# Linear attention and a two-layer network in one kernel: batch 0's numerator and denominator computed with tokens in rows, scaled there, and turned by PE

## The chip, the cores and the metric

The kernel runs on one core of a Trainium2 chip. The metric is the device time of one execution in microseconds (us). In the profile the engines are PE (matrix products; PEld is its loading of weights), DVE (element-wise work), ACT (activation functions and copies), POOL (here mostly the issue of loads) and SP (the issue of stores and of transposing transfers).

## The reference, cut to what matters

There are 8 batches of 8 heads with 576 tokens of 64 features. With phi(x) = max(x,0) + min(exp(x),1):

```python
q_p, k_p = phi(q), phi(k)
kv  = einsum('bhsd,bhse->bhde', k_p, v)
z   = sum(k_p, axis=2)
num = einsum('bhsd,bhde->bhse', q_p, kv)
den = einsum('bhsd,bhd->bhs', q_p, z)[..., None] + 1e-06
x   = (num / den), tokens in rows, heads side by side: 4608 x 512
h   = x @ w_in            # 512 x 2048
out = (h - tanh(h)) @ w_out   # 2048 x 512, float32
```

## The kernel before, in words

The order of all instructions is written out by hand; each engine runs its own list in order, and semaphores make one engine wait for another.

**Chunks and slots.** The two layers run over nine chunks of 512 tokens. For chunk `c`, layer 1 makes 16 blocks `fi` of 128 hidden features (`l1mm`, L430, four matmuls of 128x512 each, over the four pairs of heads that the 512 features of x fall into). ACT takes tanh (`th`) and DVE subtracts it, which gives `gT`. Layer 2 (`l2mm`, L451) follows in 16 slots `s` of four matmuls each. The lists `s1[fi]` and `s2[s]` hold the work of the attention that is put in behind a block or a slot, so that PE computes the attention of the next batch between the matmuls of the layers. A chunk of 512 tokens is not a batch of 576: chunk 1 begins with the last 64 tokens of batch 0 and goes on with batch 1.

**Opening.** Batch 0 has nothing to hide behind. POOL issues its loads as six halves (two halves of heads `i` for each of q, k and v), in the order q, q, k, k, v, v (L89), then w_in and w_out. For each half of q and k the phi takes three instructions (`phi_pieces`): ACT's exp `e`, DVE's `r` = max(x,0)+1, and DVE's minimum of the two, which gives `qp` or `kp`. PE turns qp (`a_qT_pe`, L166, PE transposes through PSUM; ACT and DVE each copy a part to `qT`). Then `b0_z` (L252) sums kp, `b0_kv` (L263) makes kv, and both are copied into `kz` (`b0_kz`, L267). `a_den` (L333, L337) makes den, with 1e-6 put in by matmuls with the tile `eps`; DVE takes the reciprocal (L346). `num_mm` (L273) makes num for 512 tokens with features in rows, which is how layer 1 reads x; ACT copies it to `ns` (L293). Since a den belongs to a token, hence to a column, `b0_spread` (L300) spreads the reciprocals over the rows with 32 matmuls in float32, and DVE multiplies (`b0_scale`, L304) into `xT`. Layer 1 of chunk 0 starts with the first four blocks in matmuls of 256 tokens (L686), first all four pairs on tokens 0 to 255, then on 256 to 511. `spin` (L532) multiplies zeros on PE where PE would otherwise stand still.

**The last 64 tokens of batch 0** are not needed in chunk 0. `rest_mm` (L281) and `scale_rest` (L324) make them later, in slot 8, with reciprocals that SP sends through DRAM and back (`spread_rest`).

**Batch 1** is made in layer 2 of chunk 0: phi of q at slots 0 and 1, phi of k at 4 and 5, the PE transposes at 5, `kv1` (`a_kv` L184, `a_kz`) at 8, `a_den` and `num1` (L273, L610) and the split of the reciprocals (`a_split`) at 9, `spread1` (L419, L423, four scales of 128x512) at 12. The tile `ps_all` is the whole PSUM, eight banks of 512 float32 columns; the code names banks by number.

Of the kernel before, what the change touches and what calls it, by code (L numbers as in the profile page):

```python
# [11 lines left out]
F32 = mybir.dt.float32  # L12
# [6 lines left out]
def kernel(  # L19
# [33 lines left out]
    ps_all = psum.tile([128, 8, 512], F32, name="ps_all")  # L53

# [10 lines left out]
    sel = const.tile([128, NP, 2, 64], F32, name="sel")  # L65
# [5 lines left out]
    one = const.tile([128, J * 16], BF16, name="one")  # L71
    eps = const.tile([128, 32], BF16, name="eps")
# [11 lines left out]
    def load(b, t, src, halves):  # L84

        x = src[b].rearrange("h (p j) d -> (h p) (j d)", j=J)
        if halves:
            for i in range(2):
                nc.gpsimd.dma_start(out=t[:, :, i].rearrange("q h j d -> q h (j d)"),  # L89
                                    in_=x.rearrange("(h i q) x -> i q h x", h=2, i=2)[i])  # L90
        else:
            nc.gpsimd.dma_start(out=t.rearrange("q h i j d -> q (h i) (j d)"),  # L92
                                in_=x.rearrange("(n q) x -> q n x", n=4))

    def load_k(b):
        k_t[b] = kpool.tile([128, 2, 2, J, D], BF16, name="kraw")
        load(b, k_t[b], k, b == 0)

    def load_q(b):
        q_t[b] = kpool.tile([128, 2, 2, J, D], BF16, name="qraw")  # L100
        load(b, q_t[b], q, b == 0)

    def load_v(b):
        load(b, v_b[b % 2][:, 0:2], v, b < 2)
# [45 lines left out]
    def new_qT(b):  # L150
        qT_t[b] = work.tile([128, 2, J, 2, 64], BF16, name="qT")
# [7 lines left out]
    def a_qT_pe(b, i, banks, on=None):  # L159
        if i == 0:  # L160
            new_qT(b)
        for n in range(2):
            j0, j1 = ((0, 5), (5, 9))[n]
            ps = banks().bitcast(BF16).rearrange("p (j t) -> p j t", t=128)
            for j in range(j0, j1):
                nc.tensor.transpose(ps[:, j - j0, :], qp_t[b][:, i, j].rearrange("p h d -> p (h d)"), ident)  # L166
            src = ps[:, 0:j1 - j0, :]
            dst = qT_t[b][:, i, j0:j1].rearrange("p j g t -> p j (g t)")
            if (on or "AV")[n] == "A":
                nc.scalar.copy(dst, src)  # L170
            else:
                nc.vector.tensor_copy(dst, src)
# [76 lines left out]
    def b0_z(i):  # L249

        for j in range(J):
            nc.tensor.matmul(ps_all[:, 5 - 3 * i, 0:2], kp_t[0][:, i, j].rearrange("p h d -> p (h d)"), two,  # L252
                             start=(j == 0), stop=(j == J - 1))

    def b0_zc(i):
        nc.vector.tensor_mul(kz_t[0][:, :, i, 64:96],
                             ps_all[:, 5 - 3 * i, 0:2].unsqueeze(2).to_broadcast([128, 2, 32]), mask[:, :, i, :])
# [26 lines left out]

    def b0_num(i):

        b0 = 2 * i
        num_mm(0, i, lambda h: b0 + h)

    def b0_evac(i, ns):  # L290

        b0 = 2 * i
        nc.scalar.copy(ns[:, i::2, 0:8, :].rearrange("p a j t -> p a (j t)"), ps_all[:, b0:b0 + 2, :])  # L293

    def b0_spread(pairs, n0):

        for n, p in enumerate(pairs):
            for t in range(4):
                r = slice(32 * t, 32 * t + 32)
                nc.tensor.matmul(ps_all[:, 4 + t, 128 * (n0 + n):128 * (n0 + n) + 128],  # L300
                                 sel[r, p].rearrange("p h e -> p (h e)"), rden_t[0][r, 0:128], start=True, stop=True)

    def b0_scale(p, ns, n, j0=0, j1=8):
        nc.vector.tensor_mul(  # L304
            xT[:, p, 64 * j0:64 * j1].rearrange("p (j t c) -> p t j c", j=j1 - j0, t=4),
            ns[:, p, j0:j1].rearrange("p j (t c) -> p t j c", t=4),
            ps_all[:, 4:8, 128 * n + 16 * j0:128 * n + 16 * j1].rearrange("p t (j c) -> p t j c", c=16))
# [20 lines left out]
    def a_den(b, bank, parts=range(4)):  # L328

        kz, qT = kz_t[b], qT_t[b]  # L330
        ps = ps_all[:, bank, 0:J * 16]
        for t in range(4) if b == 0 else ():
            nc.tensor.matmul(ps[32 * t:32 * t + 32], eps[:, 0:32], one[:, 0:J * 16], start=True, stop=False)  # L333
        for n, p in enumerate((0, 2, 1, 3)):
            if n in parts:
                for t in range(4):
                    nc.tensor.matmul(ps[32 * t:32 * t + 32], kz[:, p // 2, p % 2, 64:96],  # L337
                                     qT[:, p % 2, :, p // 2, 16 * t:16 * t + 16],
                                     start=(n == 0 and b > 0), stop=(n == NP - 1))
        if b > 0:  # L340
            den = rpool.tile([128, J * 16], F32, name="den")
            nc.vector.tensor_scalar(den, ps, 1e-6, None, ALU.add)
        else:
            den = ps
        rden = rpool.tile([128, J * 16], F32, name="rden")
        nc.vector.reciprocal(rden, den)  # L346
        rden_t[b] = rden
# [108 lines left out]
    def evac(c, i, o, f0=0, f1=None):  # L456
# [13 lines left out]
        def store():  # L470
            for half in range(2):
                b, j = divmod(2 * (4 * c + i) + half, J)
                cuts = [f0, 256, f1] if c == 3 else [f0, f1]
                for a0, a1 in zip(cuts, cuts[1:]):
                    nc.sync.dma_start(  # L475
                        out=out[b * S:(b + 1) * S, a0:a1].rearrange("(p j) m -> p j m", j=J)[:, j, :],
                        in_=osb[64 * half:64 * half + 64, a0:a1])
# [10 lines left out]
    load_q(0)  # L488
    make_identity(nc, ident)
    load_k(0)  # L490
    load_v(0)
# [21 lines left out]
    nc.vector.memset(one, 1.0)  # L513
# [3 lines left out]
    nc.vector.memset(eps, 0.0)  # L517
    rest = 1e-6
    for n in range(3):
        e0 = float(np.float32(rest).astype(ml_dtypes.bfloat16))  # L520
        nc.vector.memset(eps[32 * n:32 * n + 1], e0)
        rest -= e0


    for t in range(4):
        nc.vector.tensor_copy(s8[32 * t:32 * t + 32, 0].rearrange("q h p -> q (h p)"),
                              ident[32 * t:32 * t + 32, 32 * t:32 * t + 8])
    nc.vector.tensor_copy(sel, s8[:, 0].rearrange("q h p -> q p h").unsqueeze(3).to_broadcast([128, NP, 2, 64]))

    def spin(n):  # L530
        for _ in range(n):
            nc.tensor.matmul(ps_all[:, 0, :], zero[:, 0:128], zero, start=True, stop=True)  # L532
# [4 lines left out]
    for f in (eq0, rq0, mq0, eq1, rq1, mq1):  # L537
        f()
    spin(18)
    a_qT_pe(0, 0, side, "AV")  # L540
    (ek0, rk0, mk0), (ek1, rk1, mk1) = (phi_pieces(0, k_t, kp_t, "kp", i, 2 * i) for i in range(2))
    for f in (ek0, rk0):
        f()
    spin(5)
    a_qT_pe(0, 1, side, "AV")
    for f in (*ek1, mk0, rk1):
        f()
    spin(6)
    b0_z(0)
    spin(3)  # L550
    for f in mk1:
        f()
    b0_zc(0)
    b0_kv(0)
    b0_z(1)
    b0_zc(1)
    b0_kz(0)
    a_den(0, 4)
    ns0 = new_ns(0)
    spread_rest(0)  # L560
    b0_num(0)
    b0_kv(1)
    b0_kz(1)
    b0_evac(0, ns0)
    b0_num(1)
    b0_evac(1, ns0)
    b0_spread((0, 2, 1, 3), 0)
    for x in range(2):
        for n, p in enumerate((0, 2, 1, 3)):
            b0_scale(p, ns0, n, 4 * x, 4 * x + 4)  # L570

    def prepare():

        for t in range(4):
            nc.vector.tensor_copy(s8[32 * t:32 * t + 32, 1:3].rearrange("q n h p -> q (n h p)"),
                                  ident[32 * t:32 * t + 32, 32 * t + 8:32 * t + 24])
# [9 lines left out]
    for c in range(NC):  # L586
# [4 lines left out]
        if c == 0:  # L591
# [7 lines left out]
            def kv1():  # L599
                a_kv(1, 4)  # L600
                pss = rest_mm(0, 4, 256)
                a_kz(1, 4)
                scale_rest(0, pss)
# [10 lines left out]
            s2[4].append(lambda: a_kphi(1, 0))  # L614
            s2[5].append(lambda: (a_qT_pe(1, 0, Banks([4, 5])), a_qT_pe(1, 1, Banks([6, 7])), a_kphi(1, 1),
                                  load_q(2), load_k(2), load_v(2)))
            s2[2].append(prepare)
            s2[8].append(kv1)
            s2[9].append(lambda: (a_den(1, 4), num1(), spread_rest(1), a_split(1)))
            s2[12].append(spread1)  # L620
# [57 lines left out]
        if c == 0:  # L678

            first = Banks([4, 5, 6, 7, 0, 1, 2, 3])  # L680
            hs = [ps_all[:, n, :] for n in range(4)]
            for x in range(2):
                xs = slice(256 * x, 256 * x + 256)
                for n, p in enumerate((0, 2, 1, 3)):
                    for fi in range(4):
                        nc.tensor.matmul(hs[fi][:, xs], w_in_sb[:, p, fi * 128:(fi + 1) * 128], xT[:, p, xs],  # L686
                                         start=(x == 0 and n == 0), stop=(x == 1 and n == 3))
            for fi in range(4):
                l1act(fi, hs[fi], gT)
        for fi in range(4 if c == 0 else 0, NF):  # L690
            h = first() if c == 0 else ps_all[:, fi % 6, :]
            if c == 2 and fi == 1:
# [5 lines left out]
            elif c != 2 or fi > 1:  # L698
# [65 lines left out]
```

## Time and profile before

| | |
|---|---|
| Time, median of three runs | 284.41 us (284.24 to 284.88) |
| The profiled execution: its own time | 284.32 us |
| The profiled execution: span from first to last instruction | 282.6 us |
| Around the span | 1.72 us |
| PE busy | 277.0 us of the span |
| DVE, ACT busy | 176.1 and 145.6 us |
| First real matmul of layer 1 (L686) starts | 16.82 us |
| Last PE work in the chain ends | 269.00 us |

The page's first part gives the busy time of each engine. The chain of waits goes back from the last instruction to what released each step; in order of time it shows what the end hung on. A row of the timeline has start, duration, engine, line, operation, result and operand with partitions x elements, count, and in brackets the idle time before it and what ended that. A duration includes the latency of an instruction, so that in a series one starts before the one ahead has ended: the spacing is then the series' length divided by its count.

### The profile page before, as it was taken

The page shows a single profiled execution, that of the slowest core. Times are in us where ns is not written, and L with a number is a line of the kernel's source. Part 1 is how long each engine was busy: PE and PEld are TensorE (multiplying, and loading weights), DVE is VectorE, ACT ScalarE, POOL GpSimd, SP SyncE. Part 2 cuts the span into 40 slices and gives each one's busy share as a digit, 9 for nine tenths or more (in the row PEclk, how much of TensorE's full clock was granted, in tenths as well). Part 3 has the DMA queues.
Part 4 walks back from the last instruction along what each step waited for, and adds up shares of the span by engine and source line. Part 5 has one row for each costly group of instructions (what it writes and reads, how often), then busy time and mean ns, then how long its engine had stood idle before and what let it go on. Part 6 is the DMA issues. An engine that isn't in the chain of part 4 may idle for free.

```text
span 282.6 us, 5093 instructions
## 1 busy us (share of the span) xinstructions
PE 277.0 (98%) x2084; PEld 131.9 (47%) x2084; DVE 176.1 (62%) x283; ACT 145.6 (52%) x176; POOL 77.5 (27%) x69
## 2 busy tenths in 40 slices
PE   8989999999999999999999999999999999999995
PEld 3564454454444454445444444444444444444443
DVE  5859977984779773977397639764870167006600
ACT  3648647946346753566366735572651365126411
POOL 8653120430361526233614360506050000000000
PEclk9999999999999999999999999999999999999999
DMA  6999999899994399049903792252115210230032
GB/s 103 199 207 212 205 207 209 172 192 197 236 237 76 71 194 217 5 84 162 220 22 73 115 240 60 48 110 48 29 22 123 58 32 2 57 79 13 2 74 75
DMA packets 38743, 33.12 MB, mean 117 GB/s; under 512 B 16160, under 2 KB 34624, under 8 KB 38592
## 3 DMA queue, kind: packets, MB, share of 16 engines
q0 software_dynamic: 17504, 18.35, 40.1%
q1 hardware_dynamic: 21216, 14.45, 21.8%
q8 instruction: 16, 0.26, 0.3%
q14 instruction: 7, 0.06, 0.1%
HBM read 38.14 MB, written 9.46 MB: 168 GB/s over the span
## 4 chain that ended last, share of the span: by engine, by line
PE 90%; DMA 5%; POOL 1%; ACT 1%; issue 1%; SPq 0%; DVE 0%; DVEq 0%; POOLq 0%
PE ps_all L430 43%; PE ps_all L451 41%; DMA v<-in_v_dram 3%; DMA out_dram<-osb 3%; PE ps_all L184 2%; PE ps_all L273 2%; PE ps_all L686 1%; ACT osb L462 1%; SPq L475 0%; POOL kraw L89 0%; PE ps_all L337 0%; POOL qraw L89 0%; PE ps_all L300 0%; PE ps_all L166 0%; PE ps_all L263 0%
## 5 line engine op out<-in xcount | busy, mean ns | idle before, releaser
L451 PE MATMUL ps_all<-w_out_sb,gT 128*128 128x512 bf16 x560 | 124.6, 379 | 0.0
L430 PE MATMUL ps_all<-xT,w_in_sb 128*128 128x512 bf16 x560 | 122.7, 379 | 0.0
L437 DVE TENSOR_TENSOR gT<-ps_all,th 128x1024 bf16<-128x1024 f32 x64 | 77.8, 1218 | 46.4 <-ACT th L436 46.4
L436 ACT ACTIVATE th<-ps_all 128x1024 f32<-128x1024 f32 x64 | 65.5, 1024 | 46.9 <-PE ps_all L430 46.9
L430 PEld LDWEIGHTS <-w_in_sb 128*128 128x128 bf16 x560 | 54.6, 98 | 65.5
L451 PEld LDWEIGHTS <-gT 128*128 128x128 bf16 x560 | 53.8, 98 | 63.2 <-issue 0.2
L462 ACT COPY osb<-ps_all 128x512 f32<-128x512 f32 (+1 forms) x36 | 20.7, 582 | 56.4 <-PE ps_all L451 40.0
L245 POOL TENSOR_TENSOR qp<-qp,rd 128x1152 bf16<-128x1152 bf16 x10 | 21.0, 2118 | 39.1 <-issue 23.7
L231 POOL TENSOR_TENSOR pr<-qp,zb 128x1152 f32<-128x1152 bf16 x10 | 23.5, 2362 | 21.6 <-ACT zb L224 21.6
L236 DVE TENSOR_REDUCE dn<-pr 128x9 f32<-128x576 f32 x20 | 14.5, 745 | 12.2 <-POOL pr L231 12.2
L136 ACT ACTIVATE e<-qraw 128x1152 bf16<-128x1152 bf16 x16 | 18.5, 1161 | 5.4 <-DMA qraw<-in_q_dram 5.4
L136 ACT ACTIVATE e<-kraw 128x1152 bf16<-128x1152 bf16 x15 | 17.4, 1162 | 1.9 <-DMA kraw<-in_k_dram 1.9
L138 DVE TENSOR_TENSOR qp<-e,r 128x1152 bf16<-128x1152 bf16 x16 | 12.1, 759 | 4.4 <-ACT e L136 3.3
L92 POOL DMA_DIRECT2D kraw<-in_k_dram x7 | 5.4, 769 | 33.1 <-DVE r L137 17.7
L138 DVE TENSOR_TENSOR kp<-e,r 128x1152 bf16<-128x1152 bf16 x15 | 11.4, 763 | 4.4 <-ACT e L136 3.5
L441 ACT ACTIVATE th<-ps_all 128x512 f32<-128x512 f32 x16 | 9.4, 597 | 5.5 <-PE ps_all L686 3.7
L442 DVE TENSOR_TENSOR gT<-ps_all,th 128x512 bf16<-128x512 f32 x16 | 10.4, 687 | 2.7 <-ACT th L441 1.7
L532 PE MATMUL ps_all<-zero 128*128 128x512 bf16 x32 | 10.1, 475 | 1.2 <-DVE zero L485 1.2
L92 POOL DMA_DIRECT2D qraw<-in_q_dram x7 | 5.2, 741 | 16.7 <-ACT e L136 7.3
L137 DVE TENSOR_SCALAR r<-qraw 128x1152 bf16<-128x1152 bf16 x16 | 7.4, 465 | 0.4 <-DMA qraw<-in_q_dram 0.4
L460 DVE COPY osb<-ps_all 128x128 f32<-128x128 f32 x1 | 0.3, 292 | 11.6 <-DMA out_dram<-osb 11.6
L199 DVE COPY vp<-v 128x1152 bf16<-128x1152 bf16 x10 | 5.3, 525 | 3.2 <-DMA v<-in_v_dram 3.2
(105 smaller groups left out, 141.1 us busy)
## 6 DMA issues: line engine op xcount, KB each, us to landing
out_dram<-osb SPq DMA_DIRECT2D x62, 128.0 KB, 2.5
qraw<-in_q_dram POOLq DMA_DIRECT2D x7, 576.0 KB, 10.5
kraw<-in_k_dram POOLq DMA_DIRECT2D x7, 576.0 KB, 7.8
v<-in_v_dram POOLq DMA_DIRECT2D x6, 576.0 KB, 11.4
w_in_sb<-in_moe_w_in_dram POOLq DMA_DIRECT2D x3, 512.0 KB, 13.1
w_out_sb<-in_moe_w_out_dram POOLq DMA_DIRECT2D x3, 512.0 KB, 16.3
v<-in_v_dram POOLq DMA_DIRECT2D x4, 288.0 KB, 12.9
rdb<-ds SPq DMA_DIRECT2D x2, 576.0 KB
```

The costliest lines, as they stand in the source:

```text
L92: nc.gpsimd.dma_start(out=t.rearrange("q h i j d -> q (h i) (j d)"), in_=x.rearrange("(n q) x -> q n x", n=4))
L136: return (lambda: nc.scalar.activation(e, x, AF.Exp), lambda: nc.vector.tensor_scalar(r, x, 0.0, 1.0, ALU.max, ALU.add), lambda: nc.vector ...
L138: lambda: nc.vector.tensor_tensor(y, e, r, ALU.min))
L231: nc.gpsimd.tensor_mul(pr_t[b][:, i].rearrange("p j h d -> p j (h d)"), qp_t[b][:, i].rearrange("p j h d -> p j (h d)"), zb_t[b][:, i].uns ...
L236: nc.vector.tensor_reduce(dn_t[b][:, i, :, h], pr_t[b][:, i, :, h, :], mybir.AxisListType.X, ALU.add)
L245: nc.gpsimd.tensor_mul(x, x, rd[:, i].unsqueeze(2).to_broadcast([128, J * 2, D]))
L430: nc.tensor.matmul(h, w_in_sb[:, p, fi * 128:(fi + 1) * 128], xT[:, p, c * 512:(c + 1) * 512], start=(n == 0), stop=(n == NP - 1))
L436: nc.scalar.activation(th, h, AF.Tanh)
L437: nc.vector.tensor_sub(gT[:, fi:fi + 2, :], h, th)
L442: nc.vector.tensor_sub(gT[:, fi, :], h, th)
L451: nc.tensor.matmul(o, gT[:, fi, i * 128:(i + 1) * 128], w_out_sb[:, fi, :], start=(fi == 0), stop=(fi == NF - 1))
L462: nc.scalar.copy(osb[:, f0:f1], o[:, f0:f1])
```

## The change

Four things change together.

1. **Loads and phi by halves of heads.** The loads come as q, k, v of the first half, then q, k, v of the second half. `phi`, z, kv and num of the first half precede those of the second half on every engine.
2. **Batch 0's num with tokens in rows.** The matmul's weights are now 128 tokens of `qT` (whose layout for batch 0 is changed so that they lie side by side), and the moving side is 65 columns of `kz`: 64 of kv and one of z. So den comes out as the 65th column, in the same row as its token. DVE adds 1e-6, takes the reciprocal of eight numbers for each row and multiplies (`b0_scale`, four DVE instructions for two units of 128 tokens of a half of heads) into `xk`. PE turns `xk` back to features in rows (`b0_turn`, four transposes), and ACT copies to `xT` (`b0_out`). The tiles `sel`, `one`, `eps`, the reciprocal of 128x144, the spread and `ns` of batch 0 go. The first blocks of layer 1 become four parts: first half of heads, then second half. The last 64 tokens are made in the same way (`b0_rest`, `b0_rest_turn`), without DRAM.
3. **Batch 1 one slot later**: kv1 at slot 9, num1 at 10, spread1 at 13, but the PE transposes one slot earlier, at 4. Ahead of num1, in the same slot, stands `b0_rest_turn`. Chunk 1 gets the order of its first two blocks that chunk 2 had: pairs 0 and 1 for both, then pairs 2 and 3.
4. **Small**: fewer zero matmuls (25 for 32), the last block of chunk 3 is stored in two parts in place of four, batch 1's v is loaded by halves as before.

The core of the diff:

```diff
+    def tok_mm(i, js, m, bank, o):
+        for hg in range(2):
+            for h in range(2):
+                rs = slice(64 * h, 64 * h + 64)
+                nc.tensor.matmul(ps_all[0:m, bank + h, o + 65 * hg:o + 65 * hg + 65], qT_t[0][rs, i, hg, js].rearrange("p j t -> p (j t)"),
+                                 kz_t[0][rs, hg, i, 0:65], start=True, stop=True)
+    def tok_recip(m, bank, o, n):
+        d = rpool.tile([128, 2, 4], F32, name="d")[0:m, :, 0:n]
+        nc.vector.tensor_scalar(d, tok_view(m, bank, o, n)[:, :, :, 64], 1e-6, None, ALU.add)
+        nc.vector.reciprocal(d, d)
+        return d
+    def tok_scale(dst, m, bank, o, n, d):
+        nc.vector.tensor_mul(dst.rearrange("p h (x e) -> p h x e", e=64), tok_view(m, bank, o, n)[:, :, :, 0:64],
+                             d.unsqueeze(3).to_broadcast([m, 2, n, 64]))
     def b0_z(i):
         for j in range(J):
-            nc.tensor.matmul(ps_all[:, 5 - 3 * i, 0:2], ...
+            nc.tensor.matmul(ps_all[:, 7, 508:510], ...
+    def b0_scale(i, two):
+        bank, o = UNIT[i, 2 * two]
+        d = tok_recip(128, bank, o, 4)
+        for u in range(2):
+            tok_scale(xk[:, i, 2 * two + u], 128, bank, o + 130 * u, 2, d[:, :, 2 * u:2 * u + 2])
+    def b0_turn(i, two):
+        bank, c = (4 + 2 * i, (0 if two else 260) * 2)
+        for u in range(2):
+            for h in range(2):
+                nc.tensor.transpose(ps_16[:, bank + u, c + 128 * h:c + 128 * h + 128], xk[:, i, 2 * two + u, h, :], ident)
+    def b0_out(i, two):
+        nc.scalar.copy(xT[:, i::2, 256 * two:256 * two + 256]..., ps_16[:, bank:bank + 2, c:c + 256]...)
+    def b0_rest():
+        for i in range(2):
+            tok_mm(i, slice(8, 9), 64, 6, 130 * i)
+        d = tok_recip(64, 6, 0, 4)
+        tok_scale(xr[0:64].rearrange("p h i x -> p h (i x)"), 64, 6, 0, 4, d)
+    def b0_rest_turn():
+        for h in range(2):
+            for i in range(2):
+                o = 64 * (2 * h + i)
+                nc.tensor.matmul(ps_all[:, 6, o:o + 64], xr[:, h, i, :], ident[:, 0:64], start=True, stop=True)
+        nc.scalar.copy(xT[:, :, 512:576], ps_all[:, 6, 0:256].rearrange("p (a t) -> p a t", a=NP))
...
+    for f in (eq0, rq0, mq0, ek0, rk0, mk0):
+        f()
     spin(18)
+    a_qT_pe(0, 0, side, "AA")
     b0_z(0)
     b0_zc(0)
     b0_kv(0)
+    b0_kz(0)
+    b0_num(0)
+    b0_scale(0, 0)
+    for f in (eq1, rq1, mq1, *ek1, rk1, *mk1):
+        f()
+    b0_turn(0, 0)
+    spin(4)
+    a_qT_pe(0, 1, side, "AV")
+    spin(3)
     b0_z(1)
     b0_zc(1)
     b0_kv(1)
     b0_kz(1)
+    b0_out(0, 0)
+    b0_scale(0, 1)
     b0_num(1)
+    b0_turn(0, 1)
+    b0_out(0, 1)
+    b0_scale(1, 0)
+    b0_scale(1, 1)
...
             def kv1():
+                b0_rest()
                 a_kv(1, 4)
-                pss = rest_mm(0, 4, 256)
                 a_kz(1, 4)
-                scale_rest(0, pss)
-            s2[8].append(kv1)
-            s2[9].append(lambda: (a_den(1, 4), num1(), spread_rest(1), a_split(1)))
-            s2[12].append(spread1)
+            s2[9].append(kv1)
+            s2[10].append(lambda: (b0_rest_turn(), a_den(1, 4), num1(), spread_rest(1), a_split(1)))
+            s2[13].append(spread1)
...
+            some(0, 0, (0, 1))
+            some(0, 1, (0, 1))
+            b0_turn(1, 0)
+            b0_out(1, 0)
+            some(0, 0, (2, 3))
+            some(0, 1, (2, 3))
+            b0_turn(1, 1)
+            b0_out(1, 1)
+            some(1, 0, range(4))
+            some(1, 1, range(4))
```

`some(i, x, fis)` is layer 1 for the pairs of half `i`, the 256 tokens of part `x` and the blocks `fis`, in matmuls of 256 columns. `b0_num(i)` calls `tok_mm` for the four units of 128 tokens, 16 matmuls.

## The prediction

> **What bounds the kernel now.** I read the page first, then the chain of waits, then the timeline of DVE in the opening, then the groups by form for prices. All times are us from the start of the span.
>
> ```profile
> PE 277.0 (98%) x2084; PEld 131.9 (47%) x2084; DVE 176.1 (62%) x283; ACT 145.6 (52%) x176; POOL 77.5 (27%) x69
> ...
> PEclk9999999999999999999999999999999999999999
> ```
>
> PE is busy throughout and its granted clock never falls. But many of PE's early matmuls multiply zeros (L532), so the opening must be read from the chain:
>
> ```profile
> 4.80 7.41 DMA v<-in_v_dram
> 12.21 0.04 issue
> 12.25 0.48 PE ps_all L263 x36
> ...
> 13.37 0.31 PE ps_all L337 x8
> 13.68 0.34 PE ps_all L273 x4
> 14.02 0.33 PE ps_all L263 x36
> 14.35 0.02 issue
> 14.37 0.27 ACT kz L267
> 14.64 0.04 issue
> 14.69 0.41 PE ps_all L273 x4
> 15.10 1.15 PE ps_all L300 x32
> ...
> 16.34 0.43 DVE xT L304
> 16.77 0.04 issue
> 16.82 3.65 PE ps_all L686 x32
> 20.47 10.36 PE ps_all L430 x48
> ```
>
> Two things are seen. Until 12.21 the opening waits for v. From 16.82 PE runs real matmuls without a gap: 48 of L430 in 10.36 are 216 ns each, and so it goes on to 269. So whatever the change does is worth what it moves the end of L686's block (20.47), plus PE work added or stalls made after it.
>
> ```profile
> 9.91 0.42 DVE L172 COPY qT<-ps_all 128x512 bf16<-128x512 bf16 x1 [0.31 <-PE ps_all L166]
> 10.25 0.75 DVE L138 TENSOR_TENSOR kp<-e,r 128x1152 bf16<-128x1152 bf16 x1
> ...
> 13.73 1.06 DVE L346 RECIPROCAL rden<-ps_all 128x144 f32<-128x144 f32 x1 [0.22 <-PE ps_all L337]
> 16.34 2.74 DVE L304 TENSOR_TENSOR xT<-ns,ps_all 128x256 bf16<-128x256 f32 x8 [1.55 <-PE ps_all L300]
> ```
>
> DVE has idle time between 12 and 16 (1.55 in one piece); before that it is nearly full with the phi of q and k. That is the engine on which the change puts its new work.
>
> ```profile
> 6.92 1.16 ACT L136 ACTIVATE e<-qraw 128x1152 bf16<-128x1152 bf16 x1 [0.27 <-DMA qraw<-in_q_dram]
> ...
> 10.87 1.26 ACT L133 ACTIVATE e<-kraw 128x576 bf16<-128x576 bf16 x2 [0.43 <-DMA kraw<-in_k_dram]
> ...
> 13.87 0.74 POOL L112 DMA_DIRECT2D w_out_sb<-in_moe_w_out_dram  x1 [0.35 <-DMA v<-in_v_dram]
> ```
>
> **Loads.** The times at which loads land are read here from the instructions that waited for them. The six half loads of batch 0 keep their places in POOL's queue; only what they carry changes. Their landings: first 5.49 (ACT's first exp), second 6.92 (its second), third 8.6 (the first kraw issue at 3.4 plus the tile's shortest time to landing, 5.2), fourth 10.85 (exp of k's second half), fifth 12.21 (chain), sixth 13.85 (POOL's issue). So k's first half comes at 6.92 and v's first half at 8.6, but q's second half waits until 10.85 and k's second until 12.21.
>
> **First half of heads.** Exp of k 6.92 to 8.08; the minimum ends at 8.90 (before, q's second half had exactly this slot). Nine z matmuls 0.38 to 9.37. The 36 kv matmuls, 0.67 from first weights to last result as at 13.64, end at 9.95; the kz copy 0.28, 10.25. Then 16 num matmuls with 128 columns of weights and 65 moving, a form that the trace lacks: between 13 ns (L263, 0.48 for 36) and 42 ns each (L252, 0.38 for 9); I take 27, as both weights and moving side resemble L252 but half the rows are used. The changed program lets the scaling start after 8 of them: 10.7.
>
> A scaling is four DVE instructions: add and reciprocal on 128x8 (between 0.16, the small 128x8 rows of L579 to L582, and 0.22, L256 from PSUM: 0.2 each) and two multiplies of 128x256 like L304 (0.415 alone, 0.34 in a row): 1.15, with the next instruction 1.1 after its start. Bounds 0.9 to 1.4.
>
> **DVE is next.** It runs in order, and behind this scaling stands the phi of the second halves, although q's second half is there at 10.85: scaling 10.73 to 11.85; r and minimum of q 1.23 (the pitch of such a pair at 48.56 and 49.79) to 13.06; r of k 0.55; two minima of 576 (L135, 1.03 for two less overlap) to 14.45. Before, kp was complete at 12.62. Then the DVE part of the qT copy, 0.42, to 14.85. The changed program makes the second z wait for that copy too, because z now lies in bank 7, from which the copy reads.
>
> By the Trainium skill (PSUM — Partial Sum Buffer, "PSUM bank collisions raise a hardware error") two engines may not touch one bank and quadrant at once, even at other columns, so this wait is no looseness of the program; no run here shows a collision, and the 0.42 stands by L172's row alone.
>
> PE: z 14.9 to 15.28, kv to 15.75, ACT's kz 0.27 to 16.05, num (16 x 27 ns and 0.19 for the last) to 16.7, turn of tokens 256 to 511. Turns are transposes like L166: 18 in 1.17 with 219 ns for one, so 56 ns each, 0.22 for four. ACT's copy out is 128x512 bf16, near L462's 0.58: 17.05 to 17.62. Under it PE does the first four matmuls of 256 columns; the remaining 28 x 114 ns (L686, 3.65 for 32) = 3.19 and two more turns of 0.22 run from 17.67 with no further wait (scalings of the second half end at 17.7 and 18.75, their turns are due at 18.1 and 19.3): end at 21.3 instead of 20.47. **Term 1: +0.83.** It is hidden by nothing: later PE is dense. Between the bounds of scaling and num it is +0.2 to +1.4.
>
> So what is removed (eps and den matmuls 0.62, reciprocal 1.06, spread 1.15, the first scale 0.43, ACT's two ns copies 1.94) leaves the path, and the path turns to DVE's queue. The memsets and selectors removed before 5 lay beside the wait for q: nothing.
>
> The Trainium skill speaks against the turns (TensorE: Matmul & The Clock Gate, "PE-mode transpose"): about 275 ns each inside a kernel. With that, each of the two turns after 17.67 would be an estimated 1.1 instead of 0.22, and term 1 would be +2.6. L166's row disagrees with that spacing, and its 56 ns is used.
>
> **Batch 0's last 64 tokens.** Removed: rest_mm's 8 (0.06 on the chain at 40.73), six small DMAs on SP's queue and two DVE multiplies (0.48). Added on PE: 8 matmuls at 13 to 27 ns and four of 64 columns at 27 to 56: 0.2 to 0.45, I take 0.36. **Term 2: +0.3.** The DVE side (0.2 + 0.2 + 0.68, L423's size) lies under a_kv's 1.13; without that cover kz, and a_den behind it, would come up to 0.5 later.
>
> ACT's copy of these tokens (256 columns, between L267's 0.27 and L462's 0.58: 0.37) reads bank 6, which num1's first four matmuls overwrite. Between the last of the four and num1 stand the 0.45 of a_den (L337 x16); matmul latency 0.17, copy 0.37 and two handovers of 0.05 make 0.64. All of layer 2 is queued behind. **Term 3: +0.2** (0 to 0.4).
>
> **Batch 1 one slot later.** A slot is four L451, 0.86. It moves spread1 from three slots ahead of chunk 1 to two. xT's four scales (2.48 in all, 46.16 on) then end 0.95 after chunk 1's first matmul; with pairs 2 and 3 put off by four matmuls, none waits. But DVE carries the 0.86 on: gT of chunk 1 ended at 52.98 and 54.88, which is 4.25 and 6.15 after L430's start at 48.73; now 5.11 and 7.01, and banks 0/1 and 2/3 are wanted again at 24 x 0.216 = 5.18 and 32 x 0.216 = 6.91. **Term 4: +0.15** (0 to 0.4). Transposes one slot earlier: qp was ready at 34.65, slot 4 ends at 34.98; no wait. kv1 later gains nothing, it did not wait in the chain (39.60). On POOL, q of batch 1 is issued after r of q at 12.4 (12.77 before), k after 13.5 (15.48 before): no shift. Two fewer store issues for chunk 3 lie on SP beside PE.
>
> **Sum.** 0.83 + 0.3 + 0.2 + 0.15 = +1.48. The profiled execution took 284.32 (span 282.6 and 1.72 around it), 0.09 under the median of 284.41: **285.8**.
>
> **Rivals.** (1) Not slower: DVE keeps up, and v's second half at 13.85 remains the bound. This needs DVE to finish kp by 13.3, so scaling and num together to cost 1.1 less than I have. Then kv ends at 14.35, num at 15.3, ACT's copy out at 16.28, and 3.19 + 0.44 end the block at 19.95: -0.5, or 19.45 and -1.0 if the copy is not waited for. With terms 2 to 4 (0.3 to 0.65) this gives 283.6 to 284.5. For it: DVE's 1.55 idle, and first matmuls that need only half the heads. Against: the phi rows alone fill 2.6 after 10.85. (2) The clock drops: 7 of 32 spins go, and PE stands idle about a second between 11 and 12. The first zero matmuls were spaced 0.43 until 6.3, twice the later spacing; five us at half rate cost about 2.5: 288.3. Against: no gap over 1.3 in my working, PEclk full in every slice. (3) The start of chunk 1 and slot 10 stall by more, by one more operation of ACT or DVE in line there (a 0.58 copy, half a 1.22 gT): 286.8.
>
> **How the numbers follow.** Forecast 0.60 (285.0 to 286.6), rival 1 0.24, rival 2 0.06, rival 3 0.10. Some 0.2%, or 0.57, can be told from no change. Rival 1 lies half below 283.84 and half within; the forecast's low edge gives 0.04 within: faster 0.12, same 0.16, slower 0.72. The range 283.6 to 287.2 takes in rival 3, nearly all of rival 1, and leaves out the clock.
>
> **What would show it.** Right: DVE without idle from 10.7 to 14.8, the chain running through DVE's phi of the second half, the last 256-column matmul at about 21.3, layer 2 of chunk 0 stalling shortly ahead of num1. Wrong: a second kv that starts by 13.9, the block's end before 20.5, PEclk under 1, or turns spaced much over 56 ns.

## The result, and the profile after

The changed kernel takes **287.72 us** (median of 4 runs, 287.56 to 287.82) where the kernel before takes 284.37 (4 runs beside it): ratio 1.0114, 95% interval 1.0096 to 1.0131. It is slower by 3.35, and the forecast of 285.8 with its range to 287.2 is missed. The profiled execution took 287.56 (span 285.8), 3.24 more than the 284.32 of before, and its granted clock is full:

```profile
PE 273.6 (96%) x2040; PEld 131.7 (46%) x2069; DVE 177.2 (62%) x281; ACT 147.3 (52%) x180; POOL 77.9 (27%) x69
...
PEclk9999999999999999999999999999999999999999
```

PE is busy for 3.4 less than before in a longer span, so the answer is in PE's idle time. (Part of the 3.4 are zero matmuls that the change leaves out, and the trace lacks some records: 2040 matmuls beside 2069 weight loads.) First the opening, from the chain of waits (start, length, what):

```profile
10.79 0.18 DVE d L306
...
11.22 0.76 DVE xk L311 x2
...
13.21 0.69 DVE r L137
...
14.82 0.34 DVE qT L177
15.16 0.04 issue
15.20 0.36 PE ps_all L257 x9
...
17.27 0.59 ACT xT L334
...
19.82 1.75 PE ps_all L710 x16
21.57 0.05 issue
```

This is the chain that was forecast, in its order: DVE's scaling, phi of the second halves, DVE's part of qT, the second z, ACT's copy out, the block of 256-column matmuls. It ends at 21.57, not 20.47: +1.10. Next, chunk 1 in the chain, first the kernel before:

```profile
48.73 7.77 PE ps_all L430 x36
56.50 0.76 PE ps_all L184 x72
```

The changed kernel:

```profile
49.95 1.74 PE ps_all L467 x8
...
57.02 2.82 PE ps_all L467 x12
59.84 0.77 PE ps_all L189 x72
```

Chunk 1's first matmul stands at 49.95 (48.73 before): +1.22, which is 0.12 more than the opening lost. After that 2.12 are lost within chunk 1: from its first matmul to a_kv of batch 2 (L184, now L189) it takes 9.89, where it took 7.77. The sum 1.10 + 0.12 + 2.12 is 3.34, and the profiled executions differ by 3.24; the rest of the kernel gives 0.1 back. In the timeline of DVE, POOL and PE (start, busy time of the group, engine, line, tiles, count, idle time before it) the place is plain. The changed kernel:

```profile
53.11 2.72 DVE L140 TENSOR_SCALAR r<-kraw 128x1152 bf16<-128x1152 bf16 x2
55.75 1.21 DVE L474 TENSOR_TENSOR gT<-ps_all,th 128x1024 bf16<-128x1024 f32 x1
...
52.45 3.07 POOL L204 COPY vp<-v 128x1152 bf16<-128x1152 bf16 x2 [10.37 <-DMA v<-in_v_dram]
...
57.02 2.82 PE L467 MATMUL ps_all<-xT,w_in_sb 128*128 128x512 bf16 x12 [1.88 <-DVE gT L474]
```

The same two groups in the kernel before:

```profile
51.02 0.82 DVE L137 TENSOR_SCALAR r<-kraw 128x1152 bf16<-128x1152 bf16 x2
...
51.99 2.76 POOL L199 COPY vp<-v 128x1152 bf16<-128x1152 bf16 x2 [11.08 <-DMA v<-in_v_dram]
```

DVE's two r of batch 2 take 0.82 before and 2.72 after, 1.40 each in place of 0.45. Before, they ended at 51.84, 0.15 ahead of POOL's two copies of v. POOL waits for the landing of batch 2's v, which comes only 0.46 later than before (51.99, 52.45); DVE came 2.09 later, into the copies. Behind the r's stands gT, and for gT PE waits 1.88.

### The profile page after: what moved, and what is told of

Its sections match the earlier page's. It is cut to its first block, busy times and chain, and to the rows that moved or that the text cites. A ratio compares the mean times of both kernels' runs of the same rounds, so it can differ in the third digit from the quotient of the medians.

```text
span 285.8 us, 5023 instructions
## 1 busy us (share of the span) xinstructions
PE 273.6 (96%) x2040; PEld 131.7 (46%) x2069; DVE 177.2 (62%) x281; ACT 147.3 (52%) x180; POOL 77.9 (27%) x69
## 4 chain that ended last, share of the span: by engine, by line
PE 87%; DMA 4%; ACT 3%; DVE 2%; issue 2%; SPq 0%; POOL 0%; DVEq 0%; POOLq 0%
PE ps_all L467 41%; PE ps_all L488 40%; DMA out_dram<-osb 2%; DMA kraw<-in_k_dram 2%; PE ps_all L189 2%; PE ps_all L277 1%; ACT e L139 1%; PE ps_all L710 1%; ACT osb L499 1%; SPq L512 0%; DVE gT L474 0%; ACT xT L334 0%; PE ps_all L169 0%; ACT th L473 0%; PE ps_all L267 0%
## 5 line engine op out<-in xcount | busy, mean ns | idle before, releaser
L488 PE MATMUL ps_all<-w_out_sb,gT 128*128 128x512 bf16 x542 | 122.6, 379 | 1.6 <-issue 1.0
L560 PE MATMUL ps_all<-zero 128*128 128x512 bf16 x24 | 8.4, 518 | 1.2 <-DVE zero L522 1.2
L140 DVE TENSOR_SCALAR r<-kraw 128x1152 bf16<-128x1152 bf16 x15 | 8.8, 591 | 0.0
```

The source lines that it names most:

```text
L140: lambda: nc.vector.tensor_scalar(r, x, 0.0, 1.0, ALU.max, ALU.add),
L488: nc.tensor.matmul(o, gT[:, fi, i * 128:(i + 1) * 128], w_out_sb[:, fi, :], start=(fi == 0), stop=(fi == NF - 1))
```

## The experiments

The runs form three sets, each on a chip of its own with its own runs of the kernel before: 284.34 (e1 to e4), 284.23 (e5 to e8), 284.51 (e9 to e11). A ratio is the run's time over that of the kernel before, with its 95% interval. The traces taken at a mean granted clock under 0.995 (e1, e4, e10) show stretches at about half clock in the opening; the times of such executions are named with their clock, since that explains some of the scatter. In the expectations TensorE, VectorE and ScalarE stand for PE, DVE and ACT.

**e1_no_pool_copies**: the changed kernel without POOL's two copies.

```diff
-    nc.gpsimd.memset(vp[:, :, :, :, 64:66], 1.0)
...
+    nc.vector.memset(vp, 1.0)
...
-            s1[0].append(lambda: (a_vp(2, 0, nc.gpsimd), a_vp(2, 1, nc.gpsimd),
-                                  gate(qT_t[n1]), load_k(n2), load_q(n2), load_v(n2)))
+            s1[0].append(lambda: (gate(qT_t[n1]), load_k(n2), load_q(n2), load_v(n2)))
```

> The changed kernel without POOL's two copies of batch 2's v into vp (L204); vp is filled with ones at the start instead, so batch 2's kv is left uncomputed. Theory A, POOL's copies hold up DVE's two r instructions on k at the start of chunk 1 (1.40 us each there, 0.45 elsewhere): both r take 0.45, the 1.88 us of PE's idle time before gT's release goes, time about 285.7 (285.5 to 286.0). Theory B, the wait comes from DVE's backlog that the later slot hands on (0.86 us), whatever POOL does: r stays slow or PE still waits over 1.5 us, time 287.4 or more.

Measured: 286.19 (285.36 to 287.57, 8 runs), ratio 1.0054 [1.0032, 1.0077]. The three executions at full clock (0.999 to 1.0) took 285.36, 285.5 and 285.55, which is 2.0 to 2.2 less than the changed kernel's execution at full clock (287.56); the five at 0.994 or less took 286.12 to 287.57. The chain shows that the long wait at chunk 1 is gone:

```profile
50.91 7.99 PE ps_all L467 x36
58.90 0.76 PE ps_all L189 x72
```

Chunk 1 takes 7.99 instead of 9.89, so POOL's two copies cost 1.90 there. A second thing shows that the wait had covered. The profiled execution (0.994) has it in the table by stage (us and PE's busy time first, the granted clock after POOL's):

```profile
13.34:16.75 3.41, 3.41 (x59) 2.15 (x57) 2.27 (x7) 1.02 (x2) 1.39 (x2) 0.54 1.37 202
```

For 3.41 the clock is about half.

**e2_before_later_slots**: the kernel before with only batch 1 one slot later and chunk 1's first pairs reordered as in the change.

```diff
-            s2[8].append(kv1)
-            s2[9].append(lambda: (a_den(1, 4), num1(), spread_rest(1), a_split(1)))
-            s2[12].append(spread1)
+            s2[9].append(kv1)
+            s2[10].append(lambda: (a_den(1, 4), num1(), spread_rest(1), a_split(1)))
+            s2[13].append(spread1)
...
-            if c == 2 and fi == 1:
+            if c in (1, 2) and fi == 1:
```

> The kernel before with batch 1's part of the change alone: PE transposes at slot 4, kv1 at 9, num1 at 10, spread1 at 13, and chunk 1's first two blocks with pairs 2 and 3 last. Theory A: DVE's r on k moves 0.86 us later, from just ahead of POOL's copies (51.99) into them, and both r take over 1 us; PE idles 1.5 to 2.1 us in chunk 1; time 286.0 to 286.6. The prediction's term 4: +0.15, time 284.6. The opening up to L686's end stays at 20.47 in both.

Measured: 285.2 (284.99 to 285.53, 10 runs), ratio 1.0028 [1.0018, 1.0038]: +0.86, between the two expectations. Its timeline:

```profile
51.62 0.82 DVE L137 TENSOR_SCALAR r<-kraw 128x1152 bf16<-128x1152 bf16 x2
52.35 1.22 DVE L437 TENSOR_TENSOR gT<-ps_all,th 128x1024 bf16<-128x1024 f32 x1
53.49 1.65 DVE L138 TENSOR_TENSOR kp<-e,r 128x1152 bf16<-128x1152 bf16 x1
...
52.02 2.50 POOL L199 COPY vp<-v 128x1152 bf16<-128x1152 bf16 x2 [11.31 <-DMA v<-in_v_dram]
...
56.33 1.02 PE L430 MATMUL ps_all<-xT,w_in_sb 128*128 128x512 bf16 x4 [0.82 <-DVE gT L437]
```

The r's keep 0.45, and the minimum of kp is hit instead: it takes 1.65, where the same minimum took 0.85 in the kernel before (at 52.90) and the next one takes 0.74. So the later slot alone costs more than term 4's 0.15, by the same collision one instruction on. The gT between them, which reads PSUM and one SBUF tile, keeps 1.22.

**e3_pool_after_r**: the changed kernel with POOL's copies held back behind the second r by a copy of one element.

```diff
+    def pool_waits():
+        g1 = rpool.tile([1, 1], BF16, name="g1")
+        nc.gpsimd.tensor_copy(g1, r_of[2, "kp", 1][0:1, 1, J - 1, 63:64])
...
-            s1[0].append(lambda: (a_vp(2, 0, nc.gpsimd), a_vp(2, 1, nc.gpsimd),
+            s1[0].append(lambda: (pool_waits(), a_vp(2, 0, nc.gpsimd), a_vp(2, 1, nc.gpsimd),
```

> The changed kernel, complete, with one tiny POOL copy that reads the second r of batch 2's k ahead of the two copies into vp, so that POOL copies only after DVE's r. Theory A: both r 0.45 us, no wait of PE for gT; POOL's copies run from about 54.0 to 57 us, in time for kv2 at about 57.7; time 285.7 (285.5 to 286.1). Theory B: 287.4 or more. A third outcome: PE waits at kv2 for vp instead, time 286.5 to 287.5.

Measured: 286.23 (285.51 to 287.17, 5 runs), ratio 1.0055 [1.0032, 1.0078]. The profiled one (clock 0.999) took 285.51, which is 2.05 less than the changed kernel's and within 0.3 of the forecast; the other four (0.994 or less) 286.1 to 287.17. Its timeline:

```profile
52.89 0.82 DVE L146 TENSOR_SCALAR r<-kraw 128x1152 bf16<-128x1152 bf16 x2
...
54.76 0.89 DVE L147 TENSOR_TENSOR kp<-e,r 128x1152 bf16<-128x1152 bf16 x1
...
53.90 2.75 POOL L210 COPY vp<-v 128x1152 bf16<-128x1152 bf16 x2
```

Nothing is left out here and only the order of two engines differs. Not all of the 2.05 is the collision, though: in this execution the opening ended 0.22 earlier (21.35, ACT's exp of the first half of k at 6.95 instead of 7.17). In the chain chunk 1 goes as follows:

```profile
49.73 1.74 PE ps_all L473 x8
...
57.86 0.71 PE ps_all L195 x72
```

That is 8.13 instead of 9.89: the collision is 1.76 of the 2.12 lost in chunk 1, and 0.36 remain.

**e4_z_bank0**: e3 with the second z in bank 0, away from the bank that DVE's qT copy reads.

```diff
-            nc.tensor.matmul(ps_all[:, 7, 508:510], ...
+            nc.tensor.matmul(ps_all[:, 7 - 7 * i, 508:510], ...
-        nc.vector.tensor_copy(..., ps_all[:, 7, 508:510].unsqueeze(2))
+        nc.vector.tensor_copy(..., ps_all[:, 7 - 7 * i, 508:510].unsqueeze(2))
```

> The kernel of e3_pool_after_r with the second z in bank 0 in place of bank 7, so that it does not wait for DVE's copy of qT. Theory A for the opening, it hangs on DVE's list from the first scaling to kp: the second z starts 0.33 us earlier, at about 14.9, and the 256-column block ends about 0.3 earlier, at 21.3; time 0.3 under e3. Rival, the end of the block is set by PE's and ACT's own work after the turns: no change of the block's end, time as e3.

Measured: 287.25 (285.86 to 287.44, 4 runs), ratio 1.0082 [1.0052, 1.0112], with clocks of 0.988 to 0.994 in all four; the profiled one is at about half clock from 11.19 to 18.02. That hides what was to be measured: no verdict on z from this run.

**e5_pool_spins**: e3 with 8 more zero matmuls where PE idled.

```diff
     a_qT_pe(0, 0, side, "AA")
+    spin(3)
     b0_z(0)
...
     b0_num(0)
+    spin(5)
     b0_scale(0, 0)
```

> The changed kernel with POOL's copies held back behind VectorE's second r (as in e3_pool_after_r) and with 8 more zero matmuls in the two stretches where TensorE stood idle in the opening (3 ahead of the first z, 5 between num(0) and the turn). Theory: what e3_pool_after_r still has above the forecast is the half-clock stretch of 3.4 us that some executions take in the opening because TensorE idles there; kept busy, its granted clock is full in every run and all runs lie at 285.4 to 285.7, with none at 286.2 or above. Rival 1: the zero matmuls do not keep the clock; the runs scatter between 285.5 and 287.2 again, median 286.2. Rival 2: the zero matmuls delay the first z or the turn, the block of 256-column matmuls ends later than 21.35 by 0.3 or more, and the time is 285.8 or above at full clock.

Measured: 285.53, 285.58, 286.69, 286.74, all four at 0.999 to 1.0; median 286.13, ratio 1.0071 [1.0049, 1.0093]. The clock part holds: PE's busy time from 10 to 12 goes from 0.42 in the changed kernel to 1.78, and the low clocks are gone. In the table by stage, the changed kernel first, then e5:

```profile
10.00:12.00 2.00, 0.42 (x16) 0.39 (x16) 1.44 (x6) 1.13 (x1) 0.74 (x1) 1.00 1.19 192
```

```profile
10.00:12.00 2.00, 1.78 (x25) 0.97 (x25) 1.47 (x6) 1.25 (x2) 0.74 (x1) 1.00 1.19 202
```

The time did not become uniform, so half of the expectation failed: something else costs 1.1 in two of four, at full clock.

**e6_spins_alone**: the same spins in the changed kernel, collision kept (diff as e5's, on the changed kernel).

> The changed kernel with the same 8 zero matmuls and POOL's copies left where the change put them. Theory: the collision of POOL's copies with VectorE's r ends at a time set by the landing of v, so what the opening loses to the clock is hidden in the wait at chunk 1: clock full in every run, yet 287.4 to 287.6, at most 0.3 below the changed kernel. Rival: the half-clock stretch is what the changed kernel pays, and without it the time falls by 1 or more, to 286.6 or less.

Measured: 287.32 (287.23 to 287.39, 4 runs), ratio 1.0106 [1.0091, 1.0121], clock 1.0 in all. Nearly as the theory had it, 0.1 under its numbers: by the ratios the spins bring 0.0008 of 284, or 0.2, so the stretch at half clock is hardly a part of the 3.35. In the profile PE still waits 1.68 for gT in chunk 1. The end of POOL's copies comes from v's landing, so what the opening gains is lost again in the wait there. e5 differs from this run only by the copies that are held back, on the same chip: its lower two executions are 1.65 to 1.86 faster, which agrees with the 1.76 of e3.

**e7_pool_spins_z**: e5 with e4's bank 0 for the second z.

> e5_pool_spins with the second z written to bank 0 in place of bank 7, so that it does not wait for VectorE's copy of qT out of bank 7. Theory (term 1 of the forecast, which held that the second z stands behind that copy): the second z starts about 0.3 to 0.4 earlier, at 14.8 to 14.9, the block of 256-column matmuls ends at about 21.0, and the time is 0.3 below e5_pool_spins. Rival: the wait only changes its name (kp's second minimum ends as late), and the time is that of e5_pool_spins within 0.1.

Measured: 285.31 (284.86 to 286.55, 9 runs), ratio 1.0038 [1.0025, 1.005]. PE's timeline, e5 first, then e7:

```profile
15.00 0.36 PE L263 MATMUL ps_all<-two,kp 128*128 128x2 bf16 x9 [0.61 <-DVE qT L183]
```

```profile
14.34 0.38 PE L263 MATMUL ps_all<-two,kp 128*128 128x2 bf16 x9
```

z starts 0.66 earlier, the block ends as much earlier, and the profiled times differ by 0.53 (285.53, 285.0). About 0.34 of the 0.66 is the wait that was removed, as term 1 had it; the other 0.31 is DVE's r of k, which took 0.45 in this execution and 0.76 in e5's, beside POOL's issue of a load (the last section). One of the nine executions (286.55) lies near e5's upper two.

**e8_phi_first**: e7 with DVE's order changed, the second qT copy on ACT alone, the first turn behind the second kv, and the zero matmuls placed accordingly (7 more than in the changed kernel instead of 8; so also in e9 and e11).

```diff
-    spin(5)
-    b0_scale(0, 0)
-    for f in (eq1, rq1, mq1, *ek1, rk1, *mk1):
+    bank, o = UNIT[0, 0]
+    d0 = tok_recip(128, bank, o, 4)
+    eq1()
+    rq1()
+    tok_scale(xk[:, 0, 0], 128, bank, o, 2, d0[:, :, 0:2])
+    for f in (mq1, *ek1, rk1, *mk1):
         f()
-    b0_turn(0, 0)
-    spin(4)
-    a_qT_pe(0, 1, side, "AV")
-    spin(3)
+    spin(9)
+    a_qT_pe(0, 1, side, "AA")
+    spin(2)
     b0_z(1)
+    tok_scale(xk[:, 0, 1], 128, bank, o + 130, 2, d0[:, :, 2:4])
...
     b0_kz(1)
+    b0_turn(0, 0)
     b0_out(0, 0)
```

> e7_pool_spins_z with VectorE's order in the opening changed: of batch 0's scaling only the reciprocal and the first of the two products come ahead of phi of the second halves, the second product behind phi of k; the second half of qT is copied by ScalarE, and the first turn stands behind the second kv. Theory (the cost of the change at the opening is VectorE's scaling ahead of phi, 1.1, and its share of the qT copy): kp ends some 0.4 to 0.8 earlier, the block of 256-column matmuls ends at about 20.6, and the time is 284.7 to 285.1, which is the kernel before within 0.7. Rival: the chain then goes through ScalarE's copies and num's second half, the block ends at 21.0 or later, and the time is that of e7_pool_spins_z.

Measured: ratio 1.0039 [1.0024, 1.0054]. The times lie in two groups, 284.6, 284.6, 284.72, 284.84 and 285.64 to 286.26 (five), at full clock. One execution of 746.86 stands outside the comparison; nothing in the records explains it. In the profile the block ends at 20.38 in the chain, 0.09 ahead of the kernel before:

```profile
18.63 1.75 PE ps_all L722 x16
20.38 0.65 PE ps_all L473 x3
```

So the whole loss of the opening is gone. Of the 1.19 between 21.57 and 20.38, 0.21 was already gone in e5 (21.36), where the first half of k landed earlier; the other 0.98 go with z's bank, this order and an r of k at 0.45. The +0.4 to +0.6 that the better group still has against 284.23 arise later.

**e9_copies_apart**: e8 with POOL's second copy put behind DVE's first minimum.

```diff
+    def pool_waits_min():
+        g2 = rpool.tile([1, 1], BF16, name="g2")
+        nc.gpsimd.tensor_copy(g2, kp_t[2][0:1, 0, J - 1, 1, 63:64])
...
-            s1[0].append(lambda: (pool_waits(), a_vp(2, 0, nc.gpsimd), a_vp(2, 1, nc.gpsimd),
+            s1[0].append(lambda: (pool_waits(), a_vp(2, 0, nc.gpsimd)))
+            s1[1].append(lambda: (pool_waits_min(), a_vp(2, 1, nc.gpsimd),
                                   gate(qT_t[n1]), load_k(n2), load_q(n2), load_v(n2)))
```

> e8_phi_first with POOL's two copies taken apart: the first still behind VectorE's second r, the second now behind VectorE's first minimum of kp, so that at each of VectorE's two-operand-from-SBUF instructions only one copy can be in the way. Theory: the two engines take turns, an instruction of VectorE that arrives while a copy of POOL runs waits for the end of that copy (about 1.0 us each). In e5, e7 and e8 the first minimum arrives about 0.1 ahead of the end of the first copy (0.89 in place of 0.74 in the profiles), and in some executions the second copy gets in ahead of it, which costs 1.0 to 1.1; that is why the times of e8_phi_first fall in two groups, 284.6 to 284.84 and 285.64 to 286.26, at full clock. With the copies apart all runs lie in the lower group, 284.5 to 284.9. Rival: the two groups have another cause (the opening, a landing), and runs at 285.6 or above stay as frequent, 5 of 9.

Measured: 284.89 (284.49 to 285.26, 10 runs), ratio 1.0012 [1.0002, 1.0022]. None of ten lies at 285.6 or above, where five of nine did in e8. The spread is a little wider than expected, but the upper group is gone, which fits a second copy that got in ahead of the minimum. It is not shown by this alone: e8 ran on another chip and was not repeated on this one.

```profile
53.80 0.89 DVE L151 TENSOR_TENSOR kp<-e,r 128x1152 bf16<-128x1152 bf16 x1
...
52.93 1.14 POOL L214 COPY vp<-v 128x1152 bf16<-128x1152 bf16 x1
```

The copy runs from 52.93 to 54.07; the minimum, which starts at 53.80, takes 0.15 more than the 0.74 it takes alone.

**e10_old_slots**: the changed kernel with batch 1 in its old slots.

```diff
-            s2[9].append(kv1)
-            s2[10].append(lambda: (b0_rest_turn(), a_den(1, 4), num1(), spread_rest(1), a_split(1)))
-            s2[13].append(spread1)
+            s2[8].append(kv1)
+            s2[9].append(lambda: (b0_rest_turn(), a_den(1, 4), num1(), spread_rest(1), a_split(1)))
+            s2[12].append(spread1)
...
-            if c in (1, 2) and fi == 1:
+            if c == 2 and fi == 1:
```

> The changed kernel with batch 1 back in its old slots (transposes at slot 5, kv1 at 8, num1 at 9, spread1 at 12) and chunk 1's first pairs in their old order; all else of the change stays. Theory A (the later slot alone pushed VectorE's r of batch 2 under POOL's copies): the r's come 0.86 earlier and escape, 0.45 each, and the time is 285.4 to 285.7. Theory B (the slots and the late opening push alike, and the old margin of 0.15 is used up by either): the r's come at about 52.25, the first escapes and the second waits for one copy, the stall at chunk 1 is 0.3 to 1.0 in place of 1.88, and the time is 285.8 to 286.6. Theory C (the slots have no part in it): 287.3 or above.

Measured: 287.08 (287.03 to 287.29, 4 runs, clocks 0.993 and 0.994), ratio 1.0083 [1.0067, 1.01]: between the numbers of theories B and C.

```profile
52.57 2.72 DVE L140 TENSOR_SCALAR r<-kraw 128x1152 bf16<-128x1152 bf16 x2
...
56.47 2.82 PE L467 MATMUL ps_all<-xT,w_in_sb 128*128 128x512 bf16 x12 [1.01 <-DVE gT L474]
```

Both r's still meet the copies, because the opening alone (here with half clock in it; the 512-column matmuls start at 21.94) makes DVE late by more than the old 0.15. PE's wait is 1.01 instead of 1.88. So B's mechanism holds, each of the two delays brings DVE into the copies (the slot in e2, the opening here), and undoing one does not undo the collision. How much the opening alone would cost at full clock is not shown, for all four executions were at the low clock.

**e11_best**: e9 with e10's old slots, the edits above together.

> e9_copies_apart with batch 1 back in its old slots: what is left of the change is num with tokens in rows and the loads and layer 1 by halves of heads, without the second z's wait, VectorE's scaling behind phi, and no copy of POOL in VectorE's way. Theory: the block of 256-column matmuls ends 0.1 ahead of the kernel before (20.2 against 20.3 where chunk 0's 512-column matmuls start in the profiles) and chunk 1 has the old slack, so the time is that of the kernel before within 0.2, 284.1 to 284.4. Rival: the remaining tokens' turn and kv1 now crowd slots 8 and 9, TensorE stalls there, and the time is 284.6 or above.

Measured: 284.47 (284.2 to 284.78, 10 runs) beside 284.51 of before, ratio 0.9997 [0.9987, 1.0006]: no difference. Against e9 on the same chip that is 0.42 less, and chunk 1's 36 matmuls take 7.93, as in the kernel before, instead of 8.29. PE's timeline, e9 first, then e11:

```profile
48.61 8.29 PE L477 MATMUL ps_all<-xT,w_in_sb 128*128 128x512 bf16 x36
```

```profile
48.57 7.93 PE L477 MATMUL ps_all<-xT,w_in_sb 128*128 128x512 bf16 x36
```

So batch 1's later slot costs about 0.4 even without the collision. With the change's faults mended, its form of num and its loads by halves of heads bring and cost nothing that these runs can tell from zero (0.9987 to 1.0006).

## Why the prediction was wrong

**The step that failed is term 4**, batch 1 one slot later: +0.15 forecast, 2.12 measured in chunk 1. "DVE carries the 0.86 on" was right, but the term took DVE's durations from the trace of before, where the two r ended 0.15 ahead of POOL's copies. POOL's row at 51.99, with "DMA v<-in_v_dram" as its releaser, stands in that trace and is in no term: a row released by a landing does not move with DVE. DVE moved by 2.09 (51.02 to 53.11), 1.22 of it from the later chunk and the rest from the slot, and the copies by 0.46. Of the 2.12, 1.76 are the collision (9.89 against 8.13 in e3). The other 0.36 are the slot without it: 0.22 with no copies at all (7.99 in e1 against 7.77) and 0.14 more where a minimum loses as much to a copy (e3, e9). So even this part is more than twice the forecast.

The sum also took its terms as independent. Term 1 was to cost what it moves the end of the block and no more; e10 shows that the late opening brings the r's into the copies as the slot does.

**Term 1 (+0.83) was right in its mechanism**: +1.10 in the profiled execution, +0.88 in e3 with the same opening (21.35). Step by step in the profiled one: scaling from 10.79 (10.73 forecast) and 1.10 long to the next instruction (1.1); kp complete at 14.82 (14.45); the second z at 15.20 (14.9); ACT's copy to 17.86 (17.62); end at 21.57 (21.3). Two rows were longer or later than counted: the first half of k was there at 7.17, not 6.92 (in e3 at 6.95), and the r of k took 0.76, 0.87 to the next instruction, where 0.55 was counted. The trace of before has such an r too (0.68 at 7.36). One was shorter: the 16 num matmuls took 0.42 with the latency of the last, not 0.62. The turns took 0.22 for four, as taken from L166's row. The 275 ns each that the prediction weighed against it (TensorE: Matmul & The Clock Gate, "PE-mode transpose") is not the spacing of turns in a row here; one turn with its latency takes 219 ns.

**Terms 2 and 3 (+0.3 and +0.2) came to 0.12 together**, 1.22 less 1.10. The slot of kv1 with the last tokens' matmuls takes 1.25 (41.56 to 42.81), where it took 1.19 (39.60 to 40.79): +0.06. The slot of num1, from the four turns of the last tokens (43.78) to the next layer-2 matmul (45.09), takes 1.31; before, from a_den (41.76) to 43.01, it took 1.25: +0.06. For num1 already waited before, for DVE's den (0.38 between 42.21 and 42.59 in the chain). The copy of the last tokens, 0.38 at 43.94, stands in the place of that wait, not behind it. A removed wait that a new one takes over was priced as a new one. That terms 1 to 3 came to 1.22, near the forecast's 1.33, is in part luck: one was too small and the others too large.

All signs of being right that the prediction names came true (DVE without idle time to 14.8, the chain through phi of the second half, a stall ahead of num1, the block's end 0.27 after 21.3). None of them concerns chunk 1. Of its signs of being wrong, a clock under 1 came in three of the four executions, at 0.992 to 0.994.

**The rivals.** (1) needed kp by 13.3, and it came at 14.82. (2) Its clock did fall in three of the four executions (0.994, 0.994, 0.992), and "no gap over 1.3" was no argument against it: with PE busy for 0.42 of the two us from 10 to 12 the clock falls in most executions, with 1.78 in none (e5). But its price of 2.5 was not paid: the executions with the low clock took 287.66 to 287.82 against 287.56, because the wait at chunk 1 absorbs it (e6); without that wait it is 0.6 to 0.8 (e3, 286.1 to 286.3 against 285.51) and more in single executions. (3) named the right place, the start of chunk 1 and DVE in line there, and half the amount, by an additional operation instead of one that becomes three times as long.

## What to carry to other kernels

When a change shifts one engine in time, list the rows near it whose releaser is a DMA landing: they stay, and the shifted engine may now meet them. A duration read from a profile holds only with the neighbours it had there; ask for each DVE instruction with its inputs in SBUF what POOL does beside it before and after. Two delays that end in the same fixed event do not add, so undoing one of them can show little; here it took the copies, the slot and the opening together to come back to 284.47.

## What the runs showed of the hardware

**VectorE (DVE) and POOL take turns, whole instructions at a time.** A bf16 r of 1152 took 0.45 alone and 1.40 beside POOL's copies; a minimum of two SBUF tiles 0.74 and 1.65; gT, with one input in PSUM, 1.22 beside the copies (before, e2) and 1.21 to 1.22 where no copy ran (the changed kernel, e1). POOL's copy took 1.14 when a minimum followed it (e9). In the changed kernel the ends alternate: the first copy ends at 54.19, the first r 0.33 later, the second copy 1.00 after that, the second r 0.31 later, so that behind the other's end each takes no more than its own time (0.45 and 1.14). In e2 the second copy starts at 53.38 and ends at 54.52, and the minimum starts at 53.49; 54.52 plus 0.74 is 55.26, near the 55.14 at which it ended. That a second copy can also get in ahead of a minimum that already waits is argued from e8's two groups and their absence in e9; no trace of the upper group was taken. The Trainium skill (SBUF — State Buffer, "SBUF: two separate sides") has this as a rule: the port pair that the two engines share is locked for the whole of an instruction and the other is blocked. The rows here agree, and this rule, which the forecast does not use, spoke against the change.

**An r of VectorE can be longer beside POOL's issue of a load**: r of k at 13.12 took 0.76 beside the issue at 12.88 (0.74 long) in the changed kernel; in e8 the r kept 0.45 and the issue took 0.98. In e9, where the r (12.44) started ahead of the issue (12.53), neither was longer. No run left the issue out, so that it is the cause is read from these rows and not shown.

**The clock halves for stretches of 3.4 or twice that, after idle time far shorter.** 20 of the 25 executions of the versions with the short spins (the changed kernel, e1, e3, e4, e10) had a mean clock of 0.994 or less; with 7 or 8 more zero matmuls (e5 to e9 and e11) none of 47 fell under 0.998. On one chip, e10 fell in 4 of 4, e9 and e11 in none of 20. Of the kernel before, run 55 times beside them, one did (0.988, 288.61). The Trainium skill (TensorE: Matmul & The Clock Gate, Part 1) gives a window of 3413 ns, which e1's 13.34 to 16.75 agrees with, and e4's 11.19 to 18.02 with two of them (clock 0.52); its rule against idle gaps over 3.4 us ("HAM oscillation — how this bites in real kernels") is too mild here: after 6 us the longest gap of PE in the opening is 1.30 in e1 and 1.23 in e4 and e10.
